# Routed experts in a fused attention and mixture kernel: scatters through disjoint views of the output, a last block of 128 rows, one set of gathers earlier

## The chip, the cores and the metric

The kernel runs on one core of one Trainium2 chip. Its engines are PE (TensorE: matmuls; its weight loads stand apart as PEld), DVE (VectorE), ACT (ScalarE), POOL (GpSimd) and SP (SyncE, which here only issues DMAs). Each engine works through its own list of instructions in order and waits on semaphores for the others and for DMAs to land. The metric is the time of one execution on the device, in microseconds (us).

## The reference

Three stages follow one another on 1536 tokens of width 384:

```python
state = alpha[t] * state + k[t] outer v[t];  y[t] = q[t] @ state      # linear attention, 2 x 8 heads of 48
x = sum over 4 experts e of p[:, e] * (relu(x @ w1[e]) @ w2[e])       # every token through every expert
# then 8 routed experts; each token goes to its best two
noisy = x @ w_gate + log1p(exp(x @ w_noise)) * noise
top2 = argpartition(-noisy, 2)[:, :2];  w = softmax over the two
for e in range(8):
    for k in range(2):
        mask = top2[:, k] == e
        out[mask] += w[mask, k] * (relu(x[mask] @ w1[e]) @ w2[e])     # 384 -> 1024 -> 384
```

The change touches the routed experts alone. A token belongs to two of them, so two experts add into the same row of `out`; within one expert every token stands once.

## The kernel before

Every float32 product is made of three matmuls of float32r parts (high and low halves of 12 bits each), so one weight tile pair gives a row of three matmuls on PE. The stages before the routed experts (attention, four dense experts, the choice of the top two) write the experts' input rows to a DRAM scratch tensor `x2d`.

For the routed experts, lists of tokens are built on the chip. The experts are ranked by their number of tokens, and `CAPS` (line 21) gives each rank a fixed number of slots: 512, 432, 416, 404, 396, 390, 384, 380. A rank's slots are cut into blocks `s` of at most 128 rows, so rank 0 has 4 blocks, ranks 1 to 5 have three of 128 and a small rest (48, 32, 20, 12, 6 rows), rank 6 has three of 128 and rank 7 has 128, 128 and 124. In what follows "expert" means rank.

One expert `e` goes through these steps (functions from line 838 on):

- `gather(e, ...)` (line 843): one indirect DMA per block on POOL brings its rows of `x2d` into the buffer `xg{s}`, of which there is one per block number. With `prev=True` the same list brings what earlier experts have left in `out` into `pv{s}`.
- `turn(e, s)` (line 856): PE transposes a block, ACT and DVE split it into `xth` and `xtl`.
- `moe2` (line 882): eight hidden tiles of `n` columns (lines 455 to 461), then the second product. Expert 0 and those with at most 384 slots (6 and 7; `whole`, line 932) compute it block by block: 24 matmuls into one of two PSUM buffers `g2`, then `weighed`. Experts 1 to 5 compute the outputs transposed (lines 919 to 921), and `back` turns them during the next expert's hidden tiles.
- `weighed(e, s, t)` (line 869): DVE writes `yo` = product times weight plus `pv` (line 877; line 875 for expert 0), which has three buffers, and POOL scatters it to `out` by an indirect DMA (line 878). Empty slots carry an index out of bounds and are dropped.

The turns of expert `e+1` stand between the products of expert `e`. The gathers of `pv` for experts 2 to 7 are issued from inside `moe2`, after the scatters of the expert before; for expert 1 they are issued from the last loop (line 976). The Tile framework tracks who reads and writes what, and inserts the waits. All indirect accesses to `out` may touch any row, so for it each scatter overlaps every other access to `out`. POOL issues all gathers and scatters in program order; a waiting one holds up all behind it. The weights of the next expert come on SP's queue (lines 115, 120) into four `raw` buffers and are split by ACT and DVE (lines 136, 137), which is put between other work by `W.step`.

Of the kernel before, what the change touches and what calls it, by code (L numbers as in the profile page):

```python
# [19 lines left out]
# slots of the second experts: the first, then the others from the one with the most tokens  # L20
CAPS = [512, 432, 416, 404, 396, 390, 384, 380]
# [5 lines left out]
def kernel(  # L27
# [22 lines left out]
    # tokens of the attention's units, and of the first expert's  # L50
# [24 lines left out]
    class Weights:  # L75
# [28 lines left out]
        def fetch(self, i):  # L104
            e, t, g = self.order[i]
            w = self.source(e, t)
            if i < NG:
                # where the sums come later
                b0 = 2 * g if g < NG - 1 else NB - 3
                r = acc[:, b0:b0 + FG * KD * P // DM, :].rearrange("x b d -> x (b d)")  # L110
            else:
                r = wpool.tile([P, KD * FG * P], F32, tag="raw", name="raw", bufs=4)
            if t == 1:
                n = FG * P
                nc.sync.dma_start(
                    r.rearrange("p (c f) -> p c f", c=KD),
                    w[:, g * n:(g + 1) * n].rearrange("(c p) f -> p c f", p=P),
                )
            else:
                nc.sync.dma_start(  # L120
                    r.rearrange("p (c f) -> p c f", c=FG),
                    w[g * FG * P:(g + 1) * FG * P, :].rearrange("(c p) f -> p c f", p=P),
                )
            self.raw[i] = r
            if e == 0 and t == 1:
                self.whole[g] = r
# [42 lines left out]
    ones_b = const.tile([P, P], BF16, name="ones_b")  # L169
    nc.vector.memset(ones_b, 1.0)  # L170
    # the tensor engine's clock rises while the first inputs are on their way
# [25 lines left out]
    # the first rows whole, where the last block's sums come later  # L197
# [7 lines left out]
    # the first unit's keys and queries, where other blocks' sums come later  # L205
# [12 lines left out]
    def load_unit(u, names, p0=0, p1=HP):  # L218
        """The inputs of the head pairs p0 to p1 in one unit of tokens."""
        if u >= NU:  # L220
            return
        b, h0 = divmod(starts[u], S)
        hs = slice(2 * p0, 2 * p1)
        for nm in names:
            if nm == "v":
                V[u] = apool.tile([P, BM, H, D], F32, tag="v", name="v", bufs=2)
            for c in range(sizes[u] // P):
                frm = src[nm][b, hs, h0 + c * P:h0 + (c + 1) * P, :].rearrange("h p d -> p h d")
                if nm == "v":
                    nc.sync.dma_start(V[u][:, c, hs], frm)  # L230
                    continue
                nc.sync.dma_start(inputs(nm, u)[:, c, hs, :D], frm)

# [11 lines left out]
    # products of the decays that follow a step in its chunk: none after the last one  # L245
# [14 lines left out]
    def attention(u):  # L260
        """One unit of tokens, in groups of BM blocks: a block is two heads' decays and keys in one chunk."""
# [22 lines left out]
        # decays: their products from each chunk's start, and from each step to the chunk's end  # L284
# [129 lines left out]
    # the steps at which each unit's rows are done  # L414
# [30 lines left out]
    def hidden(e, f, hx, lx, t0, n, H_):  # L445
        t = ps("g1", 2)
        for kd in range(KD):
            if e == 0 and n == P:
                # too few columns for single passes
                g, o = divmod(f, FG)  # L450
                nc.tensor.matmul(t[:, :n], W.whole[g][:, (kd * FG + o) * P:(kd * FG + o + 1) * P], x32[:, kd, :],
                                 start=(kd == 0), stop=(kd == KD - 1))
                continue
            wh, wl = W.w1(e, kd, f)
            nc.tensor.matmul(t[:, :n], wl, hx[:, kd, t0:t0 + n], start=(kd == 0), stop=False)  # L455
            nc.tensor.matmul(t[:, :n], wh, lx[:, kd, t0:t0 + n], start=False, stop=False)  # L456
            nc.tensor.matmul(t[:, :n], wh, hx[:, kd, t0:t0 + n], start=False, stop=(kd == KD - 1))  # L457
        hh = wpool.tile([P, CAP], F32R, tag=f"hh{f}", name="hh")
        hl = wpool.tile([P, CAP], F32R, tag=f"hl{f}", name="hl")
        nc.scalar.activation(hh[:, :n], t[:, :n], AF.Relu)  # L460
        nc.vector.scalar_tensor_tensor(hl[:, :n], t[:, :n], 0.0, hh.bitcast(F32)[:, :n],  # L461
                                       op0=OP.max, op1=OP.subtract)
        H_[f] = (hh, hl)
# [41 lines left out]
    def drive(main, side=None, n_main=1, n_side=0, bg=None, finish=True):  # L505
        """Steps of main, with n_side steps of side to n_main of main, and bg between them."""
# [15 lines left out]
    # probabilities over their sum  # L522
# [60 lines left out]
    # keys by which the experts are ordered: the first, then by their tokens; and what they may reach  # L583
# [9 lines left out]
    # each partition's count of the tokens so far  # L593
    sofar = rpool.tile([P, E2], BF16, name="sofar")
    nc.gpsimd.memset(sofar, 0.0)
    # where the last group's tokens start among the first expert's slots: past its first two blocks
# [25 lines left out]
    def choose(g, b0, UB):  # L622
# [6 lines left out]
        # log(1 + exp(z)), with what the rounding of 1 + exp(z) takes off  # L629
# [57 lines left out]
        # the two weights  # L687
# [40 lines left out]
    def rows_of(L, n, name, pool=const):  # L728
        """Where the rows of n lists lie: for the gather (an empty slot takes row 0), and for the scatter (none)."""
# [56 lines left out]
    def the_last():  # L786
# [20 lines left out]
        # the lists in that order  # L807
# [13 lines left out]
        # an expert with more tokens than slots  # L821
# [46 lines left out]

    def weighed(e, s, t):
        """Rows of t times their weights, onto what the experts before have left there."""  # L870
# [5 lines left out]
        else:  # L876
            nc.vector.scalar_tensor_tensor(yo[:n], t[:n, :DM], wcol, PV[e, s][:n], op0=OP.mult, op1=OP.add)  # L877
        nc.gpsimd.indirect_dma_start(  # L878
            out=out, out_offset=bass.IndirectOffsetOnAxis(ap=SLOT[e * SB + s][2][:n, e * SB + s:e * SB + s + 1], axis=0),
            in_=yo[:n, :], in_offset=None, bounds_check=N - 1, oob_is_err=False)  # L880

    def moe2(e, s0, s1, aside=()):
        """One expert's rows in the blocks s0 to s1; aside is work that fits between its first products."""
# [29 lines left out]
        # the outputs on the partitions, so that no column is spent on an empty slot  # L913
# [18 lines left out]
    def whole(e):  # L932
        """Whether the blocks of an expert are so full that they need not be turned again."""
        return e == 0 or CAPS[e] <= 3 * P

# [40 lines left out]
    for e in range(E2):  # L976
        if e == 1:
            gather(e, 0, blocks(e), prev=True)
        if 0 < e < E2 - 1:
            gather(e + 1, 0, blocks(e + 1))  # L980
        drive(moe2(e, 2 if e == 0 else 0, blocks(e), back(e - 1) if e and not whole(e - 1) else ()), bg=W.step)
# [74 lines left out]
```

## Time and profile before

| what | value |
|---|---|
| median of 3 runs | 793.2 us |
| lowest, highest run | 791.04, 797.24 us |
| profiled execution: span from first to last instruction (the page gives no other time for it) | 795.4 us |
| PE busy (share of the span) | 761.2 us (96%) |
| DVE, ACT, POOL busy | 44%, 31%, 22% |
| mean granted clock of PE over the span | 0.979 |
| indirect DMAs on POOL's queue | 5.8% of the 16 DMA engines' time |

The routed experts run from about 550 us to the end. Busy time of PE is not a measure of how well it is used, but where PE stands idle the reason can be read: a timeline shows in brackets how long an engine was idle before an instruction and what ended that wait. The granted clock tells at which speed PE ran.

### The profile page before, as it was taken

Reading aid. Unit: us, or ns where it says so; the run is one execution under the profiler, and the core shown is the slowest. Engines: PE = TensorE matmul, PEld = TensorE weight load, DVE = VectorE, ACT = ScalarE, POOL = GpSimd, SP = SyncE. Lnnn points to the kernel's source line nnn. Section 1 sums busy time; section 2 is a strip of 40 time slices with the busy share of each in tenths; the row PEclk is TensorE's granted clock in tenths of the full one; section 3 lists DMA queues with packets and bytes.
Section 4 is the critical chain, followed back from the end, with each engine's and each line's share of the span. In section 5 each row is a group of like instructions: output and inputs, shape, how many; then the busy total and the mean of one; then the engine's idle time right before and its main releaser. Section 6 shows DMA issues by size and latency. Waiting matters only on the chain. (4 is left out here: it accounts for less than half of the span.)

```text
span 795.4 us, 12230 instructions
## 1 busy us (share of the span) xinstructions
PE 761.2 (96%) x4774; PEld 735.8 (93%) x4774; DVE 351.5 (44%) x856; ACT 250.2 (31%) x497; POOL 172.3 (22%) x177
## 2 busy tenths in 40 slices
PE   7999999999999999999999999888999999999793
PEld 5889999999999999999999999887989999999793
DVE  5677666663222222222222433636564474465340
ACT  2543322232311133111321331432444454444230
POOL 2420000001500023000240000435151435424331
PEclk7799999999999999999999999999999999999997
DMA  9845312100710013000121000222474466466311
GB/s 168 185 110 110 60 31 41 21 1 21 219 41 1 1 41 99 21 1 1 40 86 64 11 21 30 61 69 85 158 224 128 130 198 186 127 209 182 98 58 31
DMA packets 98382, 66.97 MB, mean 84 GB/s; under 512 B 57975, under 2 KB 94901, under 8 KB 98320
## 3 DMA queue, kind: packets, MB, share of 16 engines
q1 hardware_dynamic: 89008, 51.92, 24.9%
q0 software_dynamic: 5408, 14.12, 5.8%
q10 hardware_dynamic: 3904, 0.10, 0.4%
q8 instruction: 39, 0.64, 0.3%
q14 instruction: 23, 0.19, 0.1%
HBM read 56.68 MB, written 9.81 MB: 84 GB/s over the span
## 5 line engine op out<-in xcount | busy, mean ns | idle before, releaser
L460 ACT ACTIVATE hh<-g 128x384 fp32r<-128x384 f32 (+8 forms) x216 | 99.6, 462 | 289.2 <-PE g L457 284.6
L461 DVE SCALAR_TENSOR_TENSOR hl<-g,hh 128x384 fp32r<-128x384 f32 (+8 forms) x216 | 112.2, 520 | 169.3 <-ACT hh L460 169.1
L469 PE MATMUL g<-w2h,hl 128*128 128x384 f32 (+1 forms) x464 | 161.4, 348 | 4.1 <-DVE yo L877 4.1
L471 PE MATMUL g<-w2h,hh 128*128 128x384 f32 (+1 forms) x464 | 157.2, 339 | 0.0
L470 PE MATMUL g<-w2l,hh 128*128 128x384 f32 (+1 forms) x464 | 157.1, 339 | 0.0
L455 PE MATMUL g<-xh,w1l 128*128 128x384 f32 (+1 forms) x408 | 134.7, 330 | 1.0 <-DVE hl L461 1.0
L456 PE MATMUL g<-xl,w1h 128*128 128x384 f32 (+1 forms) x408 | 131.5, 322 | 0.0
L457 PE MATMUL g<-xh,w1h 128*128 128x384 f32 (+1 forms) x408 | 131.4, 322 | 0.0
L137 POOL TENSOR_TENSOR w1l<-raw,w1h 128x768 fp32r<-128x768 f32 x20 | 37.4, 1877 | 323.2 <-ACT w1h L136 191.2
L469 PEld LDWEIGHTS g<-w2h,hl 128*128 128x128 f32 (+1 forms) x464 | 87.7, 189 | 4.5 <-DVE yo L877 4.3
L470 PEld LDWEIGHTS g<-w2l,hh 128*128 128x128 f32 (+1 forms) x464 | 87.8, 189 | 0.0
L471 PEld LDWEIGHTS g<-w2h,hh 128*128 128x128 f32 (+1 forms) x464 | 87.5, 189 | 0.0
L455 PEld LDWEIGHTS g<-xh,w1l 128*128 128x128 f32 x408 | 76.6, 188 | 2.1 <-DVE hl L461 1.7
L456 PEld LDWEIGHTS g<-xl,w1h 128*128 128x128 f32 x408 | 76.7, 188 | 0.3 <-DVE xl L395 0.3
L455 PE MATMUL g<-xth,w1l 128*128 128x256 f32 (+7 forms) x216 | 74.4, 344 | 2.6 <-DVE hl L461 1.4
L457 PEld LDWEIGHTS g<-xh,w1h 128*128 128x128 f32 x408 | 76.6, 188 | 0.0
L498 DVE SCALAR_TENSOR_TENSOR acc<-g,prob,acc 128x384 f32<-128x384 f32 x36 | 22.2, 617 | 118.8 <-PE g L471 118.8
L456 PE MATMUL g<-xtl,w1h 128*128 128x256 f32 (+7 forms) x216 | 72.0, 333 | 0.2 <-DVE xtl L867 0.2
L457 PE MATMUL g<-xth,w1h 128*128 128x256 f32 (+7 forms) x216 | 71.9, 333 | 0.0
L878 POOL DMA_INDIRECT out_dram<-yo,si_c x26 | 28.2, 1086 | 98.0 <-DVE yo L877 47.1
L136 ACT ACTIVATE w2h<-raw 128x768 fp32r<-128x768 f32 x44 | 37.2, 845 | 34.7 <-issue 16.1
L455 PEld LDWEIGHTS g<-xth,w1l 128*128 128x128 f32 x216 | 41.4, 192 | 4.1 <-issue 1.7
(182 smaller groups left out, 1069.1 us busy)
## 6 DMA issues: line engine op xcount, KB each, us to landing
raw<-in_moe_w_dram SPq DMA_DIRECT2D x92, 384.0 KB, 3.3
v<-in_v_dram SPq DMA_DIRECT2D x12, 192.0 KB, 3.7
out_dram<-zero SPq DMA_DIRECT2D x1, 2304.0 KB, 11.3
x2d<-acc SPq DMA_DIRECT2D x12, 192.0 KB, 1.8
x_a<-in_alpha_dram SPq DMA_DIRECT2D x20, 96.0 KB, 3.2
x_k<-in_k_dram SPq DMA_DIRECT2D x18, 96.0 KB, 3.1
x_q<-in_q_dram SPq DMA_DIRECT2D x18, 96.0 KB, 3.0
acc<-in_moe_w_dram SPq DMA_DIRECT2D x4, 384.0 KB, 5.5
```

The lines of the kernel that those rows point to most:

```text
L136: nc.scalar.activation(hi, r, AF.Copy)
L137: (nc.gpsimd if e <= E1 else nc.vector).tensor_sub(lo, r, hi.bitcast(F32))
L455: nc.tensor.matmul(t[:, :n], wl, hx[:, kd, t0:t0 + n], start=(kd == 0), stop=False)
L456: nc.tensor.matmul(t[:, :n], wh, lx[:, kd, t0:t0 + n], start=False, stop=False)
L457: nc.tensor.matmul(t[:, :n], wh, hx[:, kd, t0:t0 + n], start=False, stop=(kd == KD - 1))
L460: nc.scalar.activation(hh[:, :n], t[:, :n], AF.Relu)
L461: nc.vector.scalar_tensor_tensor(hl[:, :n], t[:, :n], 0.0, hh.bitcast(F32)[:, :n], op0=OP.max, op1=OP.subtract)
L469: nc.tensor.matmul(t[:m, :DM], hl[:, o:o + m], wh, start=(f == 0), stop=False)
L470: nc.tensor.matmul(t[:m, :DM], hh[:, o:o + m], wl, start=False, stop=False)
L471: nc.tensor.matmul(t[:m, :DM], hh[:, o:o + m], wh, start=False, stop=(f == KF - 1))
L498: nc.vector.scalar_tensor_tensor(acc[:, blk, :], t[:, :DM], prob[:, blk, e:e + 1], acc[:, blk, :], op0=OP.mult, op1=OP.add)
L878: nc.gpsimd.indirect_dma_start(out=out, out_offset=bass.IndirectOffsetOnAxis(ap=SLOT[e * SB + s][2][:n, e * SB + s:e * SB + s + 1], axis=0 ...
```

## The change

Three things change.

1. `weighed` scatters block `s` through the `s`-th of four views of `out`, made by `dram_disjoint_views`, between which the framework sees no overlap. The gathers of `pv` still read `out` itself, and so stay ordered against all four views.
2. Rank 7 has 384 slots, not 380: its third block has 128 rows, not 124.
3. In the last loop, the gathers of `xg` for expert `e+1` are issued before those of `pv` for expert 1. This changes the order for `e == 1` alone.

The remaining lines of the diff take out comments, which moves the line numbers by up to five.

```diff
+from concourse.bass_types import dram_disjoint_views
...
-CAPS = [512, 432, 416, 404, 396, 390, 384, 380]
+CAPS = [512, 432, 416, 404, 396, 390, 384, 384]
...
+    parts_of_out = dram_disjoint_views(out, SB)
+
     def weighed(e, s, t):
...
         nc.gpsimd.indirect_dma_start(
-            out=out, out_offset=bass.IndirectOffsetOnAxis(ap=SLOT[e * SB + s][2][:n, e * SB + s:e * SB + s + 1], axis=0),
+            out=parts_of_out[s], out_offset=bass.IndirectOffsetOnAxis(ap=SLOT[e * SB + s][2][:n, e * SB + s:e * SB + s + 1], axis=0),
             in_=yo[:n, :], in_offset=None, bounds_check=N - 1, oob_is_err=False)
...
     for e in range(E2):
+        if 0 < e < E2 - 1:
+            gather(e + 1, 0, blocks(e + 1))
         if e == 1:
             gather(e, 0, blocks(e), prev=True)
-        if 0 < e < E2 - 1:
-            gather(e + 1, 0, blocks(e + 1))
```

How the instructions move, on POOL in three places. In the rows, `DMASW` semaphores are those of POOL's own DMAs, counted as they land; `DVE` and `PE` are those of the engines.

Between expert 0 and expert 1, before: the last two scatters of expert 0, the gathers of `pv` for expert 1, then those of `xg` for expert 2.

```order
L878 DMA out_dram<-yo,si_b 1536x384 [waits DMASW1_49,DVE_49]
L878 DMA out_dram<-yo,si_b 1536x384 [waits DMASW2_49,DVE_49]
L852 DMA pv<-out_dram,ig_c 128x384 [waits DMASW3_49]
L852 DMA pv<-out_dram,ig_c 128x384 [waits DMASW5_49]
L852 DMA pv<-out_dram,ig_c 128x384 [waits DMASW6_49]
L852 DMA pv<-out_dram,ig_c 48x384 [waits DMASW7_49]
L852 DMA xg<-x2d,ig_c 128x384 [waits DMASW0_49,PE_49]
L852 DMA xg<-x2d,ig_c 128x384 [waits PE_49] x2
L852 DMA xg<-x2d,ig_c 32x384 [waits PE_49]
```

And now:

```order
L883 DMA out_dram<-yo,si_b 1536x384 [waits DVE_49] x2
L853 DMA xg<-x2d,ig_c 128x384 [waits DMASW5_49,DMASW4_49,PE_49]
L853 DMA xg<-x2d,ig_c 128x384 [waits DMASW6_49,PE_49]
L853 DMA xg<-x2d,ig_c 128x384 [waits DMASW7_49,PE_49]
L853 DMA xg<-x2d,ig_c 32x384 [waits DMASW0_49,PE_49]
L853 DMA pv<-out_dram,ig_c 128x384 [waits DMASW3_49,DMASW2_49,DMASW1_49]
L853 DMA pv<-out_dram,ig_c 128x384 x2
L853 DMA pv<-out_dram,ig_c 48x384
```

The scatters no longer wait for one another, and the four gathers of `xg` stand ahead of the wait for the scatters to land, which now stands at the first `pv`.

Where expert 6 begins, before: the four scatters of expert 5 and the gathers of `pv` for expert 6.

```order
L878 DMA out_dram<-yo,si_c 1536x384 [waits DMASW2_49,DMASW1_49,DMASW7_49,DMASW0_49,DVE_49]
L878 DMA out_dram<-yo,si_c 1536x384 [waits DMASW6_49,DVE_49]
L878 DMA out_dram<-yo,si_c 1536x384 [waits DMASW7_49,DVE_49]
L878 DMA out_dram<-yo,si_c 1536x384 [waits DMASW0_49,DVE_49]
L852 DMA pv<-out_dram,ig_c 128x384 [waits DMASW1_49]
L852 DMA pv<-out_dram,ig_c 128x384 [waits DMASW3_49]
L852 DMA pv<-out_dram,ig_c 128x384 [waits DMASW4_49]
```

And now:

```order
L883 DMA out_dram<-yo,si_c 1536x384 [waits DMASW2_49,DMASW1_49,DMASW7_49,DMASW0_49,DVE_49]
L883 DMA out_dram<-yo,si_c 1536x384 [waits DVE_49] x3
L853 DMA pv<-out_dram,ig_c 128x384 [waits DMASW6_49,DMASW7_49,DMASW1_49,DMASW0_49]
L853 DMA pv<-out_dram,ig_c 128x384 [waits DMASW3_49]
L853 DMA pv<-out_dram,ig_c 128x384 [waits DMASW4_49]
```

The first scatter keeps its waits (for the gathers of its own expert's `pv`); the other three wait for DVE alone, and the first gather of `pv` waits for all four to land.

At the end, before: the last scatters of expert 6, the gathers of `pv` for expert 7 and its scatters.

```order
L878 DMA out_dram<-yo,si_c 1536x384 [waits DMASW5_49,DVE_49]
L878 DMA out_dram<-yo,si_c 1536x384 [waits DMASW6_49,DVE_49]
L852 DMA pv<-out_dram,ig_c 128x384 [waits DMASW7_49]
L852 DMA pv<-out_dram,ig_c 128x384
L852 DMA pv<-out_dram,ig_c 124x384
L878 DMA out_dram<-yo,si_c 1536x384 [waits DMASW1_49,DMASW2_49,DMASW0_49,DVE_49]
L878 DMA out_dram<-yo,si_c 1536x384 [waits DMASW3_49,DVE_49]
L878 DMA out_dram<-yo,si_c 1536x384 [waits DMASW4_49,DVE_49]
```

And now:

```order
L883 DMA out_dram<-yo,si_c 1536x384 [waits DVE_49] x2
L853 DMA pv<-out_dram,ig_c 128x384 [waits DMASW7_49,DMASW6_49,DMASW5_49]
L853 DMA pv<-out_dram,ig_c 128x384 x2
L883 DMA out_dram<-yo,si_c 1536x384 [waits DMASW1_49,DMASW2_49,DMASW0_49,DVE_49]
L883 DMA out_dram<-yo,si_c 1536x384 [waits DVE_49] x2
```

Again only the first scatter of an expert waits for DMAs, and the gather of 124 rows has 128.

## Rows read from the trace of the kernel before

**Rows 1.** Windows: from:to, length; busy PE, PEld, DVE, ACT, POOL; clock; DMA share; GB/s.

```profile
580.00:600.00 20.00, 18.55 (x100) 17.57 (x99) 9.38 (x14) 8.53 (x15) 10.39 (x12) 1.00 0.68 210
...
740.00:760.00 20.00, 15.93 (x86) 15.64 (x85) 7.48 (x11) 5.12 (x9) 6.68 (x7) 0.91 0.28 92
```

**Rows 2.** Waits of PE, 540 to 796: total us, times, longest.

```profile
PE g L469 <- DVE yo L877: 4.1, 1, 4.1
...
PE tr L864 <- DMA xg<-x2d,ig_c: 1.5, 1, 1.5
```

**Rows 3.** Timeline of PE near 593: start, us, operation, [idle before <-what ended it].

```profile
593.73 0.52 PE L864 MATMUL tr<-ident,xg 128*128 128x128 f32 x3 [1.45 <-DMA xg<-x2d,ig_c]
```

**Rows 4.** Timeline of POOL, 584 to 594: its gathers after expert 0.

```profile
584.21 0.99 POOL L852 DMA_INDIRECT pv<-out_dram,ig_c  x1 [3.92 <-DMA out_dram<-yo,si_b]
...
589.20 1.56 POOL L852 DMA_INDIRECT xg<-x2d,ig_c  x1 [0.30 <-issue]
```

**Rows 5.** Timeline of PE, 747 to 756: the third block of expert 6.

```profile
747.77 0.48 PE L864 MATMUL tr<-ident,xg 124*128 124x124 f32 x3
752.33 0.69 PE L469 MATMUL g<-w2h,hl 128*128 128x384 f32 x1 [4.07 <-DVE yo L877]
...
755.36 0.34 PE L469 MATMUL g<-w2h,hl 128*128 128x384 f32 x1
755.53 0.34 PE L470 MATMUL g<-w2l,hh 128*128 128x384 f32 x1
```

**Rows 6.** Timeline of DVE, 735 to 752: two sums `yo`.

```profile
735.90 0.60 DVE L877 SCALAR_TENSOR_TENSOR yo<-tr,LR,pv 6x384 f32<-6x384 f32 x1 [1.36 <-DMA out_dram<-yo,si_c]
...
751.66 0.62 DVE L877 SCALAR_TENSOR_TENSOR yo<-g,LR,pv 128x384 f32<-128x384 f32 x1 [10.06 <-DMA pv<-out_dram,ig_c]
```

**Rows 7.** Timeline of POOL, 730 to 749: scatters of expert 5, first `pv` of 6.

```profile
730.54 1.02 POOL L878 DMA_INDIRECT out_dram<-yo,si_c  x1 [4.26 <-DVE yo L877]
736.58 2.14 POOL L878 DMA_INDIRECT out_dram<-yo,si_c  x1 [5.02 <-DVE yo L877]
742.72 0.98 POOL L878 DMA_INDIRECT out_dram<-yo,si_c  x1 [4.00 <-DMA out_dram<-yo,si_c]
746.15 0.91 POOL L878 DMA_INDIRECT out_dram<-yo,si_c  x1 [2.45 <-DMA out_dram<-yo,si_c]
748.39 1.00 POOL L852 DMA_INDIRECT pv<-out_dram,ig_c  x1 [1.33 <-DMA out_dram<-yo,si_c]
```

**Rows 8.** Timeline of PE near 737: a hidden tile of expert 6.

```profile
737.03 0.44 PE L455 MATMUL g<-xth,w1l 128*128 128x384 f32 x1 [0.36 <-DVE hl L461]
```

**Rows 9.** Timeline of DVE, then POOL, 781 to 786: the last two scatters.

```profile
783.26 0.62 DVE L877 SCALAR_TENSOR_TENSOR yo<-g,LR,pv 124x384 f32<-124x384 f32 x1 [3.57 <-PE g L471]
...
781.02 1.01 POOL L878 DMA_INDIRECT out_dram<-yo,si_c  x1 [2.42 <-DMA out_dram<-yo,si_c]
784.80 1.33 POOL L878 DMA_INDIRECT out_dram<-yo,si_c  x1 [2.77 <-DVEq L1024]
```

**Rows 10.** DMA issues, us to landing; windows from 780.9, 784.7, 724.3, 771.3.

```profile
out_dram<-yo,si_c POOLq DMA_INDIRECT x1, 2.9
...
out_dram<-yo,si_c POOLq DMA_INDIRECT x1, 6.2
...
xg<-x2d,ig_c POOLq DMA_INDIRECT x1, 9.2
...
pv<-out_dram,ig_c POOLq DMA_INDIRECT x1, 5.4
```

**Rows 11.** Line 1051 (the kernel's end): ns min/median/max, first and last start us.

```profile
L1051 POOLq DRAIN  x3: 46/112/9214, 785.3 to 795.1; - x3
```

**Rows 12.** SP's queue, ACT, DMA issue, 722 to 729: weight pieces of expert 7.

```profile
723.00 3.57 SPq L115 DMA_DIRECT2D raw<-in_moe_w_dram  x4
...
727.90 0.84 ACT L136 ACTIVATE w1h<-raw 128x768 fp32r<-128x768 f32 x1
...
raw<-in_moe_w_dram SPq DMA_DIRECT2D x2, 384.0 KB, 4.3
```

## The prediction

> **What bounds the kernel now.** I read the page first: PE is busy for 96% of the span, so a transfer or an engine beside it counts only where PE waits for it, or behind PE's last matmul. Then the windows of the routed experts: PE has full stretches except from 580 to 600 us, where 18.55 of 20 us are busy, and from 740 to 760, where 15.93 are, with a mean granted clock of 0.91 [rows 1]. (Part of the first gap can be matmul records that are missing, so I go by waits, not by busy time.) The list of PE's waits names two long ones there: 4.1 us for a sum `yo` and 1.5 us for gathered rows `xg` [rows 2]. The timelines show how each came about, and a third small one. Last I read the end, where PE has finished and one scatter is still to land.
>
> **The gathers moved ahead (change 3).** PE waits 1.45 us at 593.73 for the first block of `xg` of expert 2 [rows 3]. POOL issued that gather at 589.20, behind four gathers of `pv` of which the first went out at 584.21 after 3.92 us of waiting for expert 0's last scatter [rows 4]. With the four `xg` ahead, the first needs only its buffer, whose reader on PE ran before expert 1 began. It can go at 584.21 minus 3.92, near 580.3, some 9 us sooner, and the wait goes: **-1.45 us**. What is late instead: the `pv` gathers of expert 1 now stand behind four issues, each 1.56 us at most [rows 4] plus 0.3 between two, so the first goes at about 587.7 and the last lands some 10 us later. They are wanted by sums that DVE makes while expert 2's hidden tiles run, after 600; nothing waits for that.
>
> **The scatters through views (change 1).** The four scatters of expert 5 went out at 730.54, 736.58, 742.72 and 746.15, the last three after the one before had landed, and `pv` of expert 6 at 748.39, after the fourth [rows 7]. Its first block let DVE make `yo` at 751.66, after 10.06 us of waiting [rows 6], and PE, which needed the PSUM buffer that this sum empties, stood for 4.07 us until 752.33 [rows 5]. After the wait PE ran slowly: from 752.33 to 755.36 are nine steps in 3.03 us, 0.34 each, against 0.17 for the next [rows 5]. That is the lower of its two levels, 1.2 GHz for 2.4, and cost 3.03 - 9 x 0.17 = 1.5 us more.
>
> With the change the fourth scatter waits for its sum alone. That sum ended at 736.50 [rows 6], and it keeps its own wait of 1.36 us, since it takes the `yo` buffer of the first scatter, which must have landed. So the fourth goes out near 736.8. How long it takes to land with three in flight no row shows; scatters took 2.9 us alone and 6.2 us at worst [rows 10]. Then `pv` goes out between 739.7 and 743.3 and not at 748.39, and the first `yo` is ready by 751.66 + 0.62 - 5.1 = 747.2 at the latest. PE wants the buffer behind the transposes of 747.77 [rows 5], so even this end leaves it time. I take the whole wait and the slow steps: **-5.6 us**; the end of no gain is a rival below.
>
> The wait of 1.36 us for a `yo` buffer held DVE, and a hidden tile's low part behind it, and PE stood for 0.36 us at 737.03 [rows 8]. The first scatter landed late behind the gather of 124 rows, which took 9.2 us [rows 10]; that gather now has 128 rows. Between 0 and 0.36 I take **-0.4 us**, since the sum misses its time by 1.36 us and the gather by more. In experts 1 to 4 the scatters also waited for one another, but PE did not wait, so earlier scatters are worth nothing there: the cover is the hidden tiles of the next expert, and without it each expert would cost what expert 6 does.
>
> **The last block (change 2).** Behind PE's last matmul come a sum that ends at 783.26 + 0.62 = 783.88, a scatter issued at 784.80 [rows 9], and its landing 6.2 us later, at 791.0; the scatter of 128 rows just before it landed in 2.9 us [rows 10]. Nothing else moved then. The gather of 124 `pv` rows took 5.4 us [rows 10], so the slow landing is a pattern of the 124-row forms. With views the scatter goes out about 0.3 us behind its sum, the usual step between POOL's issues [rows 4], 0.6 us sooner; and it lands in between 2.9 us (a 128-row scatter) and 6.2 us (no change). I take 2.9, its nearest neighbour in form and time: 3.3 + 0.6 = **-3.9 us**. The added columns cost 72 hidden matmuls x 0.17 us x 4/384 = **+0.1 us** at PE's step of [rows 5]; ACT and DVE get 1% longer tiles beside PE.
>
> The Trainium skill speaks against this part: its page "DMA: Bandwidth & Descriptors", section "Anatomy of one DMA — SWDGE (gpsimd) path", fits such a DMA by 2.0 us plus its bytes over 436 GB/s, which as an estimate gives 2.4 us for 124 rows and as much for 128; by that the edit is worth nothing and the sum is 787.5. The 6.2 us of the 124-row scatter contradicts it. The same page, section "Why a DMA increments its semaphore by 16 and not by 1", says that a transfer runs on the largest number of DMA engines up to 16 that divides its slowest dimension: 4 for 124, 16 for 128. The trace's 6.2 against 2.9 us agrees with this one.
>
> **Sum.** -1.45 - 5.6 - 0.4 - 3.9 + 0.1 = -11.2 us. Against the profiled span of 795.4 us this gives **784.2 us**. That execution lies 2.2 us above the median of 793.2, so it may hold a longer wait than the median run does; against the median the same sum would give 782.0.
>
> **Rivals.**
>
> *The end does not shorten* (0.25). For it: POOL's closing instruction takes 9.2 us from 785.3 [rows 11], to 794.5, long after the landing at 791.0. If it counts from its own start and not from the landing, the 3.3 us are lost. Equally if the slow landing has another cause than the rows, as the page's fit would have it. Against: the two short DRAINs of 0.05 and 0.11 us in the same row had no transfer in flight, so the long one probably waits for one. Time: 784.2 + 3.3 = 787.5.
>
> *The wait moves from the scatters to the queue* (0.12). Four transfers in flight beside weight pieces may land as late as the slowest indirect DMA here, 9.2 us [rows 10]. Then `pv` goes out at 736.8 + 9.2 + 0.3 = 746.3, 2.1 us sooner than now, PE still waits about 2.0 us and pays the 1.5 us of slow steps: 784.2 + 3.5 = 787.7. Against: the slow gather is one of the 124-row forms.
>
> *Slower: the weights come late* (0.04). The first piece of expert 7's weights, issued at 723.00, landed 4.3 us later, and ACT used it at 727.90 [rows 12], 0.6 us after. ACT is in order and evicts hidden tiles behind it, so PE stops when the piece comes later. If scatters and gathers in flight together hold these pieces back by d, six boundaries lose 6 x (d - 0.6). That outweighs the gain from d = 2.5 us on; at a doubled landing (d = 4.3) it gives 784.2 + 22 = 806. Against: the same bytes move, POOL's DMAs take 5.8% of the DMA engines' time, and the gathers move away from these loads, to earlier times.
>
> *The views change nothing* (0.02): then 784.2 + 6.0 + 0.6 = 790.8. The order of POOL's waits speaks against it. Two of the rivals together (0.02) give about 791.
>
> **Numbers.** The forecast has 0.55. Its own bounds are 782.0 (the sum against the median) less 2 us of run spread at the low end; the high end takes in both rivals at 787.5 and 787.7 with the same 2 us: 780 to 790. A change of 1% is about what a measurement of this kernel can tell from none; faster by that much means under 785.3. The forecast is under it in four of five cases, and the first rival is at it when taken against the median: faster 0.55. Slower needs over 801: 0.04. The rest is within 1%: 0.41.
>
> **What would show it.** In the changed profile PE's list has no wait for `xg` near 593 and none for `yo` near 748, and no steps at 0.34 us behind it; three scatters of expert 5 follow their sums within 0.3 us; the last scatter lands in about 3 us, and the span ends some 7.3 us after that scatter's issue, not 10.6. A wait for `yo` that stays, of a length with the landing of expert 5's last scatter, speaks for the queue; a closing DRAIN of 9 us for the first rival; waits of ACT for `raw` for the slower one.

## The result and the profile after

The changed kernel took 786.25 us (median of four runs, 785.72 to 787.36) where the kernel before took 795.22 us beside it (791.04 to 797.79): a ratio of 0.988, with a 95% interval of 0.985 to 0.991. The forecast of 784.2 us was 2 us too low; its range and its direction held. The profiled span fell from 795.4 to 785.6 us, 9.8 us where 11.2 were forecast.

The runs of the kernel before spread by 7 us; the second profile of it, below, shows where 4.1 us of that lie.

The page and the waits of PE from 540 us on in the changed kernel (columns as in [rows 2]):

```profile
span 785.6 us, 12222 instructions
...
PE 760.1 (97%) x4774; PEld 734.3 (93%) x4774; DVE 351.6 (45%) x856; ACT 250.1 (32%) x497; POOL 170.1 (22%) x177
```

```profile
PE tr L865 <- DMA xg<-x2d,ig_b: 1.8, 1, 1.8
PE g L456 <- DVE hl L462: 1.5, 3, 0.8
PE g L456 <- ACT xth L867: 0.6, 1, 0.6
PE g L457 <- DVE xtl L868: 0.2, 1, 0.2
```

Both long waits of [rows 2] are gone; the first line is a wait for expert 1's rows near 555, which the kernel before has too. The windows of [rows 1] are now full, at full clock:

```profile
580.00:600.00 20.00, 20.00 (x108) 18.95 (x106) 9.66 (x14) 8.66 (x15) 11.51 (x12) 1.00 0.67 211
740.00:760.00 20.00, 20.00 (x119) 19.94 (x118) 9.23 (x14) 6.84 (x12) 8.34 (x8) 1.00 0.27 86
```

PE's timeline at the three places of [rows 3, 5, 8], and its last matmul, in the changed kernel:

```profile
591.67 0.36 PE L926 MATMUL g<-hh,w2h 128*128 128x432 f32 x1
591.87 0.49 PE L865 MATMUL tr<-ident,xg 128*128 128x128 f32 x3
...
735.15 0.44 PE L456 MATMUL g<-xth,w1l 128*128 128x384 f32 x1 [0.38 <-DVE hl L462]
...
745.89 0.49 PE L865 MATMUL tr<-ident,xg 128*128 128x128 f32 x3
746.14 0.42 PE L470 MATMUL g<-w2h,hl 128*128 128x384 f32 x1
...
775.35 0.34 PE L472 MATMUL g<-w2h,hh 128*128 128x384 f32 x1
```

And in the kernel before, the matmul ahead of the wait of [rows 3], and the last one:

```profile
591.92 0.36 PE L921 MATMUL g<-hh,w2h 128*128 128x432 f32 x1
...
782.88 0.34 PE L471 MATMUL g<-w2h,hh 128*124 128x384 f32 x1
```

These times split the gain by place, against the same instructions before:

| stretch | before | after | difference |
|---|---|---|---|
| start to the transposes behind 591 | 593.73 | 591.87 | -1.86 |
| from there to the transposes of expert 6's third block | 154.04 | 154.02 | 0.0 |
| from there to PE's last matmul | 35.11 | 29.46 | -5.65 |
| from there to the end of the span | 12.5 | 10.2 | -2.3 |

Of the 1.86 us, 1.61 are the wait that is gone: 1.45 us of idle time, and the rest of the step that it cut off. The other 0.25 (591.92 against 591.67) lie ahead of 562, where no edit acts: the changed kernel came to 556 about 1 us later, and the kernel before ran from 556 to 562 at a mean granted clock of 0.72, the changed one at 1.00. The 0.38 at 735.15 is the small wait of [rows 8]: it stayed.

POOL, first between experts 0 and 1, then around expert 5's scatters (before: [rows 4, 7]):

```profile
580.35 0.99 POOL L853 DMA_INDIRECT xg<-x2d,ig_c  x1 [0.30 <-PE g L456]
...
585.34 1.69 POOL L853 DMA_INDIRECT pv<-out_dram,ig_c  x1 [0.30 <-issue]
...
728.64 1.02 POOL L883 DMA_INDIRECT out_dram<-yo,si_c  x1 [10.70 <-DVE yo L882]
729.97 1.01 POOL L883 DMA_INDIRECT out_dram<-yo,si_c  x1 [0.31 <-issue]
732.46 0.98 POOL L883 DMA_INDIRECT out_dram<-yo,si_c  x1 [1.48 <-DVE yo L882]
734.93 1.80 POOL L883 DMA_INDIRECT out_dram<-yo,si_c  x1 [1.50 <-DVE yo L882]
740.14 1.00 POOL L853 DMA_INDIRECT pv<-out_dram,ig_c  x1 [3.40 <-issue]
```

The gather for expert 2 goes out at 580.35, 8.9 us sooner than at [rows 4]. The four scatters go out within 6.3 us (15.6 in [rows 7]), each behind its sum, and `pv` for expert 6 follows 8.3 us sooner. DVE's sums there, and the last one (before: [rows 6, 9]):

```profile
734.02 0.60 DVE L882 SCALAR_TENSOR_TENSOR yo<-tr,LR,pv 6x384 f32<-6x384 f32 x1 [1.38 <-DMA out_dram<-yo,si_c]
743.99 0.62 DVE L882 SCALAR_TENSOR_TENSOR yo<-g,LR,pv 128x384 f32<-128x384 f32 x1 [4.29 <-DMA pv<-out_dram,ig_c]
...
775.73 0.62 DVE L882 SCALAR_TENSOR_TENSOR yo<-g,LR,pv 128x384 f32<-128x384 f32 x1 [3.58 <-PE g L472]
```

The sum that PE waited for now ends at 744.61; PE wants its buffer behind the transposes of 745.89, and its next matmul is at 746.14, so 1.5 us are left. The fourth sum still waits 1.38 us for a buffer whose scatter, the first, landed in 5.3 us, the first line below. The second line is the last scatter's landing (DMA issues, us to landing; windows from 728 and 776.5; before: [rows 10]):

```profile
out_dram<-yo,si_c POOLq DMA_INDIRECT x1, 5.3
...
out_dram<-yo,si_c POOLq DMA_INDIRECT x1, 3.2
```

The last scatter and POOL's closing DRAIN, the one long instruction that ends its queue (before: [rows 9, 11]):

```profile
776.62 0.98 POOL L883 DMA_INDIRECT out_dram<-yo,si_c  x1 [3.19 <-DVE yo L882]
```

```profile
L1056 POOLq DRAIN  x3: 46/113/7556, 777.2 to 785.3; - x3
```

The scatter went out 0.27 us behind its sum (0.92 before) and landed in 3.2 us, not 6.2: 3.0 us sooner. The span ends 9.0 us behind the issue, where it ended 10.6 behind: only 1.6 of the 3.0 us came through, since the DRAIN still took 7.6 us (9.2 before).

### The profile page after: what moved, and what is told of

Its sections match the earlier page's. It is cut to its first block, busy times and chain, and to the rows that moved or that the text cites. A ratio compares the mean times of both kernels' runs of the same rounds, so it can differ in the third digit from the quotient of the medians.

```text
span 785.6 us, 12222 instructions
## 1 busy us (share of the span) xinstructions
PE 760.1 (97%) x4774; PEld 734.3 (93%) x4774; DVE 351.6 (45%) x856; ACT 250.1 (32%) x497; POOL 170.1 (22%) x177
## 4 chain that ended last, share of the span: by engine, by line
PE 68%; issue 14%; POOL 7%; DVE 4%; DMA 4%; ACT 1%; POOLq 0%; DVEq 0%; ACTq 0%
PE g L470 9%; PE g L472 9%; PE g L471 9%; PE g L456 9%; PE g L457 9%; PE g L458 9%; POOL pv L853 2%; PE tr L279 2%; PE sc L371 2%; POOL xg L853 2%; DMA out_dram<-yo,si_c 2%; PE sc L331 2%; POOL out_dram L883 2%; PE sc L345 1%; PE sc L367 1%
## 5 line engine op out<-in xcount | busy, mean ns | idle before, releaser
L461 ACT ACTIVATE hh<-g 128x384 fp32r<-128x384 f32 (+7 forms) x216 | 99.4, 461 | 288.1 <-PE g L458 283.6
L462 DVE SCALAR_TENSOR_TENSOR hl<-g,hh 128x384 fp32r<-128x384 f32 (+7 forms) x216 | 112.3, 521 | 168.6 <-ACT hh L461 168.4
L470 PE MATMUL g<-w2h,hl 128*128 128x384 f32 x464 | 161.0, 347 | 0.0
L472 PE MATMUL g<-w2h,hh 128*128 128x384 f32 x464 | 156.9, 338 | 0.0
L471 PE MATMUL g<-w2l,hh 128*128 128x384 f32 x464 | 156.7, 338 | 0.0
L471 PEld LDWEIGHTS g<-w2l,hh 128*128 128x128 f32 x464 | 87.5, 189 | 0.0
L470 PEld LDWEIGHTS g<-w2h,hl 128*128 128x128 f32 x464 | 87.3, 188 | 0.2
L472 PEld LDWEIGHTS g<-w2h,hh 128*128 128x128 f32 x464 | 87.2, 188 | 0.0
L456 PE MATMUL g<-xth,w1l 128*128 128x256 f32 (+6 forms) x216 | 73.9, 342 | 2.6 <-DVE hl L462 1.5
L457 PE MATMUL g<-xtl,w1h 128*128 128x256 f32 (+6 forms) x216 | 71.3, 330 | 0.2 <-DVE xtl L868 0.2
```

The source lines that it names most:

```text
L470: nc.tensor.matmul(t[:m, :DM], hl[:, o:o + m], wh, start=(f == 0), stop=False)
L471: nc.tensor.matmul(t[:m, :DM], hh[:, o:o + m], wl, start=False, stop=False)
L472: nc.tensor.matmul(t[:m, :DM], hh[:, o:o + m], wh, start=False, stop=(f == KF - 1))
```

## The experiments

All times are compared with runs of the kernel before on the same chip.

### Each part alone

The views alone:

```diff
-            out=out, ...
+            out=parts_of_out[s], ...
```

> The kernel before with the scatters through disjoint views and nothing else. My theory: the only wait of PE that the views take away is the one behind expert 5's four scatters, near 748 us, 4.1 us long with 1.5 us of half-speed steps behind it, and at the end the last scatter goes out 0.3 us behind its sum (0.6 us sooner); so the span falls by about 6 us against the kernel before, PE's wait of 1.5 us for xg near 593 stays, and the last scatter of 124 rows still lands in about 6 us. Rival: the views help in every expert, since each saved wait on POOL brings the next gathers forward; then the wait near 593 shrinks too and the fall is 7 us or more. Second rival: the end comes out the same because the last scatter sets it by its slow landing alone; then the fall is 5.6 us at most.

790.6 us (789.9 to 792.8) against 797.6, ratio 0.993 [0.990, 0.996]. The wait for `yo` is gone, the one for `xg` stays at 1.8 us, the last scatter lands in 6.0 us, and the span is 788.9: the theory held.

The 384 slots alone:

```diff
-CAPS = [512, 432, 416, 404, 396, 390, 384, 380]
+CAPS = [512, 432, 416, 404, 396, 390, 384, 384]
```

> The kernel before with the last expert's third block of 128 rows, not 124, and nothing else. My theory: the last scatter lands in about 3 us, not 6.2, and the gathers of that block likewise; PE's wait of 4 us near 748 stays as it is, since expert 5's scatters still follow one another; the span falls by 1.6 us (the closing DRAIN gives back part of the 3 us), at most by 3.3. Rival, as I had it in the prediction: the 124-row gather of xg delays expert 5's first scatter and with it the whole chain; then the first scatter lands about 2 us sooner, PE's wait near 748 shrinks to about 2 us, and the span falls by 3.5 to 5 us.

790.3 us (788.7 to 794.0), ratio 0.992 [0.988, 0.995]: as much as the views. The prediction gave the slots no part in the stop near 748. PE's waits from 540 on in this kernel:

```profile
PE tr L864 <- DMA xg<-x2d,ig_b: 1.7, 1, 1.7
PE tr L864 <- DMA xg<-x2d,ig_c: 1.5, 1, 1.5
PE g L469 <- DVE yo L877: 1.4, 1, 1.4
```

The wait for `yo` has shrunk from 4.1 to 1.4 us with no slow steps behind it, although the four scatters still wait for one another. Neither theory had this: the first scatter landed in 5.0 us, only 0.2 us sooner than before.

The gathers alone:

```diff
+        if 0 < e < E2 - 1:
+            gather(e + 1, 0, blocks(e + 1))
         if e == 1:
             gather(e, 0, blocks(e), prev=True)
-        if 0 < e < E2 - 1:
-            gather(e + 1, 0, blocks(e + 1))
```

> The kernel before with the gathers of the third expert's rows ahead of those of the second's sums, and nothing else. My theory: PE's wait of 1.5 us for xg near 593 goes and nothing else moves, so the span falls by 1.5 us, which the timed runs can hardly tell from none. Rival: the gathers of the second's sums, now behind the four others, come so late that the sums of the second expert and their scatters are late too; then POOL's first scatter near 614 waits for a DMA, and the fall is under 1 us or a rise.

796.4 us (790.5 to 797.8), ratio 0.999 [0.997, 1.002]. In the profile (span 794.4) the wait near 593 is gone and the one for `yo` is 4.1 us as before. A gain of 1.45 us is within what the runs can tell.

The change without the 384 slots:

```diff
-CAPS = [512, 432, 416, 404, 396, 390, 384, 384]
+CAPS = [512, 432, 416, 404, 396, 390, 384, 380]
```

> The changed kernel with the last expert's third block of 124 rows as before. My theory: no wait of PE near 593 or 748, the last scatter goes out 0.3 us behind its sum and lands in about 6 us, not 3.2; the span is longer than the changed kernel's by 1.6 us if the closing DRAIN of POOL ends 3.5 us after the landing or 7.5 us after its own start, whichever is later, and by 3 us if it ends a fixed time after the landing. Rival: the slow landing of the 124 rows was due to what the kernel before had in flight and not to the row count; then the landing is about 3 us and the span as that of the changed kernel.

788.6 us (787.4 to 789.6), ratio 0.990 [0.987, 0.993], span 785.7; both waits are gone with the 124 rows in place. That the span is as short as the changed kernel's says nothing of the slots: this execution was 0.9 us ahead at 560 already and had no small wait near 735, and from PE's last matmul to the end it took 11.9 us, not 10.2. The medians of the three parts alone add up to 7.0 + 7.3 + 1.2 = 15.5 us, the whole change gave 9.0 (beside other runs of the kernel before): views and slots take away the same stop.

### What the stop near 748 is made of

The kernel before once more:

> The kernel before once more, for a second profile of it: its times spread from 792 to 798 us in the comparisons. Theory: the spread is the wait near 748 with its slow steps (5.6 us together); an execution near 797 has both, one near 792 has neither or only the wait. Rival: the wait near 748 is there in both and of the same length, and the spread comes from waits elsewhere, such as ACT's at 637 to 641.

This execution took 792.8 us, its span is 791.0. POOL's timeline and PE's, as in [rows 7, 5]:

```profile
730.67 1.02 POOL L878 DMA_INDIRECT out_dram<-yo,si_c  x1 [3.19 <-DVE yo L877]
736.43 1.01 POOL L878 DMA_INDIRECT out_dram<-yo,si_c  x1 [4.73 <-DVE yo L877]
739.86 0.98 POOL L878 DMA_INDIRECT out_dram<-yo,si_c  x1 [2.43 <-DVE hl L461]
743.33 0.91 POOL L878 DMA_INDIRECT out_dram<-yo,si_c  x1 [2.48 <-DMA out_dram<-yo,si_c]
745.56 1.01 POOL L852 DMA_INDIRECT pv<-out_dram,ig_c  x1 [1.32 <-DMA out_dram<-yo,si_c]
```

```profile
747.62 0.48 PE L864 MATMUL tr<-ident,xg 124*128 124x124 f32 x3
749.55 0.44 PE L469 MATMUL g<-w2h,hl 128*128 128x384 f32 x1 [1.45 <-DVE yo L877]
749.82 0.34 PE L470 MATMUL g<-w2l,hh 128*128 128x384 f32 x1
750.01 0.34 PE L471 MATMUL g<-w2h,hh 128*128 128x384 f32 x1
```

The second scatter makes the difference. In [rows 7] its issue took 2.14 us and it landed 5.4 us after its start; here 1.01 and 2.7 us. All behind it moves by some 2.8 us, and PE waits 1.45 us instead of 4.07. Behind the long wait PE took its steps 0.34 us apart [rows 5]; behind the short one they are 0.18 apart. PE's last matmul comes 4.12 us sooner than in the first profile (778.76 against 782.88): 2.62 of wait and 1.5 of slow steps. So the theory held for these two executions: the kernel before runs in a long and a short form, and the forecast's -5.6 us was worked out from the long one. Against the short one the change gains 791.0 - 785.6 = 5.4 us.

What makes an issue long can be narrowed down. The fourteen traces of this case hold 1201 indirect issues of POOL. Of these, 103 took over 1.35 us: three are of 122 rows, and each of the other 100 ran in part beside a conversion of weights on DVE (128x768 elements). Of the 1098 shorter ones 198 did. Here is the conversion beside the second scatter, in the long form and then in the short one:

```profile
736.90 0.94 DVE L137 TENSOR_TENSOR w1l<-raw,w1h 128x768 fp32r<-128x768 f32 x1
```

```profile
736.75 0.94 DVE L137 TENSOR_TENSOR w1l<-raw,w1h 128x768 fp32r<-128x768 f32 x1
```

It began 0.32 us behind the issue in both. So such a conversion stands beside every long issue of this kind, but it does not decide alone; no run takes it away.

The views for experts 1 to 4 alone:

```diff
-            out=out, ...
+            out=parts_of_out[s] if 0 < e < 5 else out, ...
```

> The kernel before, with the views for the scatters of experts 1 to 4 alone; expert 5's still wait for one another. Theory A (PE's wait near 748 belongs to expert 5's own chain of scatters): the wait stays at about 4 us with the slow steps behind it, and the time is within 2 us of the kernel before, near 796; then the views of experts 1 to 4 and the views of expert 5 are each worth nothing in time, and it takes both. Rival B (the chain of the earlier experts makes the queue late, and holds up the weights' conversion as at 637 to 641 us in the kernel with the views in expert 5 alone): the earlier experts' views carry the gain, the time is near 791, and PE's wait near 748 is under 1 us.

792.2 us (789.7 to 793.4, ten runs) against 798.2, ratio 0.994 [0.991, 0.997]. Of the kernel before, 11 of 13 runs beside these took 796 us or more. PE's wait:

```profile
PE g L470 <- DVE yo L880: 1.4, 1, 1.4
```

Neither theory had it whole. Expert 5's own chain costs 1.4 us, as in the short form; the other 2.6 us and the slow steps go when the scatters of the earlier experts stop waiting (the second scatter's issue took 1.01 us). How is not shown. The gathers behind those scatters end sooner: the last `xg` for expert 6 is issued at 719.24 here and at 724.32 in [rows 10]'s 9.2 us case, and lands in 5.8 us. But with the 384 slots alone it went out at 724.72, and in the second profile of the kernel before at 725.52, where it took 8.6 us to land, and the wait was the short one there too.

The views for expert 5 alone, twice:

```diff
-            out=out, ...
+            out=parts_of_out[s] if e == 5 else out, ...
```

> The kernel before, with the views for expert 5's four scatters alone; all others name the whole output as before. Theory (the gain in the middle is worth what one expert's last scatter holds up): PE's wait for a sum near 748 and the half-speed steps behind it go, as with the views everywhere (4.1 + 1.5 us); the wait for gathered rows near 593 stays (about 1.5 us, as with the views alone), and the last matmul to the end takes what it took in the kernel before, about 12.5 us, since the last scatter still waits for its predecessor. Span about 795.4 - 5.6 = 789.8, against 788.9 for the views everywhere. Rival (scatters of the other experts count too): the wait near 748 shrinks but stays above 1 us, because the queue is still late from the chain of earlier experts; span above 792.

> The kernel with the views in expert 5 alone, for a second profile. In the first, the wait near 748 was gone, but ACT stood for 2.96 us before a conversion of weights at 639.81, and PE lost some 5 us near 641 and 674. Theory (the serial scatters of experts 2 to 4 push the gathers into the time in which weights are converted, so that stop is part of this kernel): it recurs, span near 796. Rival (a single disturbance, perhaps of the profile): it does not recur, and the span is near 790.

The wait for `yo` is gone in both profiles, as the theory had it. But the first time this kernel took 797.0 us (794.9 to 799.5, ten runs), ratio 0.999 [0.996, 1.002], with a span of 796.7; the second time, in a single run on another chip, 792.1, with a span of 790.2. The first profile lost its time elsewhere:

```profile
639.81 0.85 ACT L137 ACTIVATE w2h<-raw 128x768 fp32r<-128x768 f32 x1 [2.96 <-remote]
...
670.38 0.85 ACT L137 ACTIVATE w2h<-raw 128x768 fp32r<-128x768 f32 x1 [2.19 <-PE g L924]
```

ACT stood before two conversions of weights, and PE, which waited for ACT's `yT` behind them, lost some 6 us against the second profile near 641 and 674, in waits and slow steps. The second profile has nothing of it, as the rival had it. What held ACT is open: records of semaphores are missing in that trace between 636 and 641, but the piece that the first conversion needed had landed at 625.8, so it was no late weight. Which of the ten runs had it nothing shows. But each of them lies at least 2.7 us above the 792.1, so in the timed runs the views for expert 5 alone gained nothing, although they take the wait away.

### The small wait that stayed

```diff
-        yo = mp["p"].tile([P, DM], F32, tag="yo", name="yo", bufs=3)
+        yo = mp["p"].tile([P, DM], F32, tag="yo", name="yo", bufs=4)
```

> The changed kernel with four buffers for the sums instead of three. Theory (the small wait that stayed near 735 comes from the fourth sum of expert 5, which waits on DVE for the buffer of the first scatter, and that scatter lands 5.3 us late among the weight pieces): DVE's wait of 1.38 us before its sum at 734.02 goes, and PE's gap of 0.55 us behind it, so the span is some 0.4 us shorter, 785.2 against 785.6, which is inside what the runs can tell. Rival (the gap is PE's own, or the transfer's lateness shows elsewhere): the gap near 735 stays at 0.5 us or more and the span does not move.

787.3 us (786.5 to 788.0), ratio 0.987 [0.983, 0.991], span 785.9. The fourth sum no longer waits, and PE has no wait there:

```profile
732.55 0.61 DVE L882 SCALAR_TENSOR_TENSOR yo<-tr,LR,pv 128x384 f32<-128x384 f32 x1
733.08 0.55 DVE L462 SCALAR_TENSOR_TENSOR hl<-g,hh 128x384 fp32r<-128x384 f32 x1
733.54 0.60 DVE L882 SCALAR_TENSOR_TENSOR yo<-tr,LR,pv 6x384 f32<-6x384 f32 x1
```

So DVE's wait was for the buffer of the first scatter. That PE's small wait comes from DVE's shows in the profiles taken together: PE waited 0.36 to 0.6 us in the three in which DVE waited 1.36 us or more, and 0.2 us at most in the others, in which DVE waited up to 1.2 us. The worth, 0.38 us, is below what the runs can tell, and the total did not move; this is no better version.

### The end

The changed kernel without expert 7's scatters:

```diff
+        if e == E2 - 1:
+            return
         nc.gpsimd.indirect_dma_start(
```

> The changed kernel without the three scatters of expert 7; its output lacks that expert's part. It asks what POOL's closing DRAIN waits for. Theory (the DRAIN ends a set time, some 8.1 us, behind the issue of the last scatter, so that a landing sooner than 4 us buys nothing): with the last scatter then 50 us or more earlier, the DRAIN is as short as the other two, under 1 us, and the end lies some 3 us behind PE's last matmul, span near 778. Rival (the DRAIN has a fixed length from its own start, however long ago the last transfer): it still takes 7.5 us, the span depends on when POOL reaches it.

Its closing DRAIN and POOL's last transfer, now a gather for expert 7:

```profile
L1058 POOLq DRAIN  x3: 46/113/8826, 760.0 to 778.3; - x3
```

```profile
761.04 0.95 POOL L853 DMA_INDIRECT pv<-out_dram,ig_c  x1 [0.30 <-issue]
```

The DRAIN was not short: it took 8.8 us, from 760.0 to 768.8, 7.8 us past the last issue, but beside PE's work. The span (778.6) ends 2.7 us behind the last matmul (775.90), not 10.2. So the scatter at the end costs 7.5 us in all. The theory failed on its condition: the gathers for expert 7 are still issued up to 761.04, so the DRAIN had a fresh issue beside it, and it ended 7.8 us behind that, where the theory has 8.1. The rival's fixed length is not there either, 8.8 us against 7.6. The DRAIN's start and the last issue lie only 1 us apart, so what it counts from stays open.

122 and 120 rows in the last block:

```diff
-CAPS = [512, 432, 416, 404, 396, 390, 384, 384]
+CAPS = [512, 432, 416, 404, 396, 390, 384, 378]
```

> The changed kernel with 378 slots in the last expert, so that its last block has 122 rows. By the rule that a transfer is spread over the largest number of DMA engines up to 16 that divides its rows, 122 rows go over 2 engines, 124 over 4 and 128 over 16. Theory: the last scatter lands later than with 124 rows (6.2 us), 9 us or more, and the span ends some 3.9 us behind that landing: about 785.6 + 3 to 6 = 789 to 792. Rival (only whole blocks of 128 rows are quick, whatever divides the rest): it lands in about 6.2 us as 124 rows do, and the span is that of the changed kernel with 124 rows, 785.7 to 787.

```diff
-CAPS = [512, 432, 416, 404, 396, 390, 384, 384]
+CAPS = [512, 432, 416, 404, 396, 390, 384, 376]
```

> The changed kernel with 376 slots in the last expert, so that its last block has 120 rows. 122 rows ended 3.9 us behind a landing of 7.4 us. Theory (what counts is the divisor: 120 rows go over 15 DMA engines): the last scatter lands in about 3 us, the closing DRAIN ends 8.1 us behind that scatter's issue as with 128 rows, and PE's last matmul to the end takes 10.2 us; span about 785.6. Rival (only whole blocks of 128 rows are quick): the landing takes 6 us or more and the end lies 11.7 us or more behind PE's last matmul.

The closing DRAIN (same line form as in [rows 11]) and the last scatter with 122 rows, then with 120:

```profile
L1056 POOLq DRAIN  x3: 46/113/10843, 778.5 to 789.9; - x3
```

```profile
777.99 1.71 POOL L883 DMA_INDIRECT out_dram<-yo,si_c  x1 [3.26 <-DVE yo L882]
```

```profile
L1056 POOLq DRAIN  x3: 46/113/7629, 777.1 to 785.3; - x3
```

```profile
776.59 1.03 POOL L883 DMA_INDIRECT out_dram<-yo,si_c  x1 [3.20 <-DVE yo L882]
```

The changed kernel with 380 slots, for comparison:

```profile
L1056 POOLq DRAIN  x3: 46/113/9242, 775.6 to 785.4; - x3
```

The spans are 790.2 us with 122 rows and 785.6 with 120, from one run each. With 120 rows the scatter landed in 3.2 us, as with 128, and its theory held; with 122 its landing is not recorded, and the table goes by the last packet of POOL's queue, whose 7.4 us lie between the 9 us of that theory and the 6.2 of its rival; the span is within the theory's 789 to 792.

| rows of the last block | kernel | last packet ends behind the issue | DRAIN | issue to the span's end |
|---|---|---|---|---|
| 128 | changed | 2.7 us | 7.6 us | 9.0 us |
| 120 | changed, 376 slots | 2.8 | 7.6 | 9.0 |
| 124 | changed, 380 slots | 5.8 | 9.2 | 10.6 |
| 124 | before | 5.8 | 9.2 | 10.6 |
| 122 | changed, 378 slots | 7.4 | 10.8 | 12.2 |

Eight rows less are as quick as 128, four or six less are slower: it is the divisor, not the nearness to 128. The packets that the last scatter is cut into go the same way: 64 with 128 and 120 rows, 192 with 124, 352 with 122. In the slow cases the DRAIN ends 3.9 us behind the last packet; in the quick ones that would be 6.7 us behind the issue, but it ends at 8.1. So both hold: a length that the landing can't shorten, and a landing that can lengthen it. Of all traces that end with a scatter, in the nine with 124 or 122 rows the DRAIN ends 3.9 us behind the last packet, and in the four with 128 or 120 rows 8.1 us behind the issue, whether the last packet came 2.1 or 3.1 us behind it.

## Why the prediction was right, and where it was not

**The base.** The 784.2 us were worked out from a span and read as a time. A run's time lies above its span, by 1.8 us in the changed kernel's profiled run (787.36 against 785.6), so of the first three runs of the kernel before only the one of 797.24 us can be the profiled one: it lay 4.0 us above the median of 793.2, not 2.2. In spans the sum missed by 1.4 us, and its parts missed by more, as follows.

**The gathers (-1.45 us): right.** The wait is gone in the changed kernel and with this edit alone, by the step named: the first `xg` went out at 580.35, where 580.3 was forecast, and `pv` at 585.34; nothing waited for it. The stretch got 1.6 us shorter by it.

**The views near 748 (-5.6 us): right in size, narrower in cause than told.** The stretch got 5.65 us shorter, and the first `pv` went out at 740.14, within the 739.7 to 743.3 that were forecast. I read the 4.07 us as one chain of four landings. The runs split it: 1.4 us are that chain, which stays with views for experts 1 to 4 alone and goes with views for expert 5; 2.6 us, and the 1.5 us of slow steps that came with them, are one scatter whose issue took 2.14 us, in most runs, by their times, and not in all. That part also goes with the 384 slots alone or with views for the earlier experts alone. So the step "earlier scatters are worth nothing there" failed: no wait of PE shows in experts 2 to 4, but views for experts 1 to 4 alone gave 6.0 us. How they and the slots act on that one issue, and what made it long, is not shown. The caution that the profiled execution might hold a longer wait than others was right; but as the exception it was wrong: in two comparisons 26 of 33 runs of the kernel before took 796 us or more (in the third 13 of 17, with times up to 809.55). It is because the profiled execution was like most that the size came out right.

**The 0.36 us near 737 (-0.4): failed.** The step blamed the gather of 124 rows. With it at 128 rows and landing in 3.0 us the wait stayed, 0.38 us. The first scatter of expert 5 landed in 4.2 to 5.5 us in every profile in which it was recorded, with 124 or 128 rows, with weight pieces in flight beside it in the kernel before and in the changed one; no run takes these away. The fourth buffer took the wait away.

**The end (-3.9 us): mis-sized, -2.3.** The 0.6 us for the sooner issue came (0.92 to 0.27 behind the sum), and the landing fell as the divisor has it, to 3.2 us where 2.9 was taken. But the term let all of the 3.3 us through to the end, where 1.6 came: the span ended 9.0 us behind the scatter's issue, where 7.3 was forecast. The argument against the first rival, that the short DRAINs had no transfer in flight, was half the truth: by an estimate from the table, a last packet later than 4.2 us (8.1 - 3.9) behind the issue sets the end, and with a sooner one the 8.1 us do. The span of 785.6 us lies between the forecast's 784.2 and this rival's 787.5.

The Trainium skill's page "DMA: Bandwidth & Descriptors", section "Why a DMA increments its semaphore by 16 and not by 1", gives 16, 15, 4 and 2 DMA engines for 128, 120, 124 and 122 rows, and the four DRAINs of 7.6, 7.6, 9.2 and 10.8 us stand in that order. By the fit in the section "Anatomy of one DMA — SWDGE (gpsimd) path" of the same page of the Trainium skill, as an estimate, all four would land alike. The table speaks against that.

**The added columns (+0.1 us)** are too small to be seen. **The queue** and **the weights** as rivals did not come: the fourth scatter landed in 4.4 us and left 1.5 us of slack, and no wait for `raw` appeared in the changed kernel.

Taken together, -1.6 - 5.65 - 2.3 and 0.25 ahead of 562 make the 9.8 us of the two profiles; the last is luck, since no edit acts there.

## What to carry to other kernels

A chain of small transfers that wait for one another can matter where no engine waits for it: here taking apart the earlier experts' chains alone gave 6.0 us, by a way that stays open. Where runs spread, a second profile is due before a wait is priced (the same wait, with its slow steps, was worth 5.6 us in one execution and 1.45 us in another). A quicker last transfer is worth only what the program's closing instruction passes on: read that instruction's length against the landing. Choose the row counts of indirect transfers by their divisors: 128 rows (16 x 8) and 120 (15 x 8) landed in 2.5 to 3.2 us at the end of this kernel, 124 (4 x 31) in 6.0 to 6.2, and the last packet of 122 (2 x 61) came after 7.4.

## What was not expected of the hardware

- POOL's closing DRAIN took 7.6 us behind a scatter that landed in 3.2, and 8.8 us in the run whose last POOL transfer was a gather 15 us ahead of PE's end. It never ended sooner than 7.8 us behind POOL's last issue.
- The same gather of 128 rows landed in 3.0 us ahead of the weight pieces (issued at 716.99 in the changed kernel) and in 7.0 us among them (at 724.72 with the 384 slots alone); 0.66 us of the difference are the longer issue.
- Of the 103 indirect issues that took POOL over 1.35 us, all but three of 122 rows ran beside a conversion of weights on DVE.
